# The low halves of w_in formed on TensorE instead of VectorE, in a re-planned order (mLSTM, gated MLP and routed attention on one core)

## The chip, the cores and the metric

The kernel runs on 1 core of one Trainium2 chip. The metric is the time of one execution in microseconds of device time; of the kernel before there are three timed runs. On the core, TensorE multiplies matrices into PSUM, VectorE (DVE), ScalarE (ACT) and GpSimd (POOL) work on tiles, and SyncE (SP) and ScalarE issue the loads. Each engine runs its own instructions strictly in order and waits on semaphores for the others.

## The reference, cut to what matters

Three layers in a row, on 4 batches of 768 positions.

```
# 1 mLSTM, 8 heads of 40: per step t
m_new = maximum(f + m, i)                   # gates in log space
C = exp(f + m - m_new) * C + exp(i - m_new) * outer(v, k);  n likewise with k
y = sigmoid(o_gate) * (C @ q) / maximum(|n . q|, 1)
# 2 gated MLP over x = y (320 wide), w_in 320 x 1024, w_out 512 x 320
u, v = split(relu(x @ w_in))                # 512 each
v_n = (v - mean) / sqrt(var + 1e-6)
gated = u * (w_spatial @ v_n + b_spatial);  x2 = gated @ w_out
# 3 four attention experts of 64, two chosen per position, causal softmax
out = sum over the chosen of w_e * (softmax(q k^T / 8) @ v) @ wo[e]
```

All arrays are float32. The change concerns `w_in` alone.

## The kernel before, in words

The sequence is cut into 24 tiles of 128 positions (4 batches of 6). For each there is an mLSTM chunk (`mlstm`, with `m_decay`, `m_value`, `m_state`), a normalization (`norm`, which multiplies by the v half of w_in) and an attention tile (`attend`). The gated MLP (`gmlp`) and the projections (`qkv`) work on units of one to three tiles.

Products that need more than float16 precision are made of two float16 halves: an array `t` is kept as `hi = float16(scale * t)` and `lo = float16(scale * t - hi)`, and three products stand for one. The weights get their halves in the kernel. `w_in` and `w_out` come as 8-byte words and are made into float32 by three bit instructions of VectorE (`load_f64`, tile `u`); then `split_w` makes the halves: a cast on an engine chosen by a letter (`sw`), then one subtraction on VectorE (`less`), which writes the low half.

```
    def split_w(k, t, hi, lo, scale, tag="vn"):
        yield on("sw", k)
        on("sw", k).cast(hi, t, scale)
        yield dve
        x = P - lo.shape[0]
        less(lo, t[x:], hi[x:], scale)
        flow.done(tag)
```

The ten pieces of w_in have the numbers k = 0 to 9. Pieces 0 to 7 go straight into the tile `wi` (256 columns each). Pieces 8 and 9 hold the last 64 rows of w_in packed on 128 partitions; their halves go to the tile `ee`, and four loads each by SP carry them from there into `wi`.

The order of the work is written out by hand: every coroutine (a thread such as PM3 for `mlstm(3)` or PI4 for a piece of w_in) yields the engine of its next step, and the table ORDER says which thread goes on next. The instructions of each engine come out in that order. The table CFG has one letter per step for steps that more than one engine can do: v for VectorE, a for ScalarE, p for GpSimd. All instructions are recorded in one helper, so they carry line 154 in the profile, and are told apart by their tiles. `g` is a PSUM bank (four, and two lent ones), `qs` and `qkT` are the stacked queries and keys and their transpose, `dd` the decay matrix, `cf` and `cs` the mLSTM state and its halves, `wx` and `vx` the values, `wsT` the halves of w_spatial, `qkst` early on the halves of the other weights, `vn` loads and normalized values, `u` the assembled float32 pieces and later the first half of the MLP. The first product of VectorE with the gate (`u<-pst,u`) needs the normalized tiles of the whole first batch.

Of the kernel before, what the change touches and what calls it, by code (L numbers as in the profile page):

```python
# [20 lines left out]
P = 128  # L21
# [172 lines left out]
class Flow:  # L194
# [106 lines left out]
    def run(self):  # L301
# [20 lines left out]
    qt="vaaaaaaavaaa",  # L322
    fe="p",
    ic="a",
    cc="aaaa",
    nc="aava",
    gk="vaaa",
    gt="av",
    rz="p",
    bh="pa",  # L330
    sw="avaaapapaaapvvapapaaavvappapvaapapa",
    qkh="ppavaaaaaapvvaaaaaaaaaaaavppppaaaaapavaaaaaaaaaa",
    wf="vvvvp-vvvvv-ppvvp-vvvvv",
    wh="pvaaa-avaaa-aaapa-avvap",
    wl="pvvvp-vvpvv-vpvpv-ppvpp",
    ch="aaaaa-vaava-papaa-vaaaa",
    cl="vvvpp-vvvvv-vvppv-pvvvp",
    cm="-vpvv--pppv--pvvv--vvpp",
    y="vvpvvvvvvvvvpvvppvpvvpvv",
    x1h="apvaaavavavvppavpaaaavvv",  # L340
    x1l="vvvvvpvvvppvppvvpvpvvvvv",
    w2="avavaaaa",
    vnh="aaaaavvpapvaaaaaaaaavaaa",
    ru="vvaavavvavaaaavavaaaavvvaaavavvvvaav",
    vh="------avvavaaaapaaavavva",
    Wh="------------aaaaaaaapaapaaaaaaavaaaaaaaaaaaaaaaa",
    gh="aapaapppvaaaaaaaavvvavppvvvvpapvvppa",
    qh="vavaaaaaaavvaaavvvaavvvaaaaavaaaaaaa",
    vvh="avvavvvavavaavvvvaaaaavv",
    rt="pppvvvpvp",  # L350
    ah="aaaaaapaappvavaaaaapaaapapvvaaavvapapvvpaapvaaaavvpvavavaaaavppppavvpaaapaapvaapavpvvaappavpvpav",
    osh="aavvaaapaaaapapvvaappppv",
    res="aaaavvaavvavavavvvvvavaa",
# [6 lines left out]
    al="ppppvvppvvvpppvvvvvppvvvvvvvpppvpvvvvvvpvvvvpvpvvppppppvvvvvvppvvvpppvppvppppvpppvpvvppvppvppvpv",  # L360
    co="ppppvvpvvvpppvpppvpvppvp",
    dn="ppvvpvvvppvpppppppvppvpv",
    gl="vvppvvpvvpvppvvvvpvpvvpvvvpvpppvvvpp",
    osl="ppvvvvvvvppppvppppppvvvv",
    pc="vpvvaa",
    pl="pp-vv",
    r3="vpvvppppp",
    r4="ppvppvppp",
    se="vpppvppvpvppvppvppvppppv",
    vnl="pppvvpvvpvpvvpppvvpvpppv",  # L370
# [15 lines left out]
FW6 PK1 FH7 PL4 FM2 PS1 PS0 FW7 PN1 PS0 FW7 PS3 PM3 FM2 PN1 FM3 PI1 PS2 PK1 PM5 PS2 FS11 PM3 PN0 PK2 FS11 PL4 PM5
PK0 PM3 FS10 PM2 PN0 PM3 PV4 PV5 PT4 FM3 FX11 PM3 FS10 PM3 PK1 FX11 FX10 PR0 PD4 FH8 PI0 FX10 FH9 PM3 PK3 PM3 PD4
PI0 FH9 PM5 PK4 PL6 FM5 PM3 FH8 PK0 FH9 PM3 PM3 PK3 FH8 PK2 PV4 PM3 FW8 PK4 FW9 PV4 PN2 FW8 PL5 PR0 FM3 FW9 PM3 PN1
FM3 PK2 PS0 FM4 PS5 PK3 PM6 PM4 PG1 FS13 PI0 FM4 PN2 FS12 FS13 PN2 FS12 PM4 PI0 PL5 PN0 FM4 PN3 PU0 PM6 PM4 PU0 PK4
PN1 PM4 FG0 PG1 PM4 PN3 PM4 PD5 PM4 PM4 FH10 FH11 PS3 PL7 PG1 FH10 PM4 PD5 FH11 PS0 FG1 PM4 PM4 FH10 FG0 FM4 FH11  # L390
PG1 PN3 FW10 PM4 FW11 FG2 PT5 PN2 FW10 PL6 PR0 FW11 PM4 FM4 PN2 PM5 PS1 PN2 PM7 PG1 PN3 FG1 FS14 FG2 PG1 PS5 PM5
FS15 FG0 FS14 PM5 PN2 FG3 PV6 PT6 PL6 PM5 PN3 PG1 PM5 PS2 FS15 PU0 PG1 PM5 PR0 PM7 FP6 PM5 PS2 FG3 PD6 PM5 FH12 FH13
FP6 FT1 FH12 PD6 PM5 FG1 FH13 FT1 FH12 PM5 PN3 FH13 PM5 FW12 PL8 PV6 FW13 PM5 FW12 PN4 PV6 FW13 FW12 PL7 PV6 FW13
FW12 PM5 FG0 PR0 FW13 FG1 PN4 PG1 FR6 PN3 PM6 PN4 PG1 FM6 PM6 PN4 FG3 PM6 FG0 PM6 PM6 PM8 FG2 PN4 PM6 PV7 PN5 PL7
PM6 FS17 FP7 FU3 PM6 PM6 FS16 PM6 PN4 FS16 FG1 PL8 PG1 PU1 FP7 FG3 FM6 PM6 PS3 PN5 FG2 PD7 PN4 FH14 FH15 PG1 FG1
FH14 PV7 PD7 FG2 FU4 FH15 FM6 FH14 FG3 PN5 FS17 FW14 PG1 FH15 FG2 FW14 PN5 FW15 FG0 PL8 FW14 FW15 PN6 PM8 FW14 FW15
FM6 PN5 PG1 FG3 PT7 PV7 FW15 PN6 PD8 FH16 PN5 FR7 FH16 PM7 PV7 PL9 PN5 FH17 FU5 PM7 FH17 PD8 FG3 FH16 PM7 PN6 FM7
FH17 PM7 PG1 FG3 PV8 FP8 PM7 FW16 PM7 PG1 FP8 FG1 FW16 FM7 FG2 PM7 PV8 FW17 FG3 PM7 FG2 PV8 FG4 FW16 PM7 FM7 PV8 PM7
# [103 lines left out]
def mlstm_gmlp_moe(ctx: ExitStack, tc, qkvo, i_gate, f_gate, w_in, w_in3, w_sp, b_sp, w_out, w_out3, wqkv, wo, out):  # L502
# [33 lines left out]
    def on(what, x):  # L536
        return flow.pick(what, x)
# [124 lines left out]
    def first(it):  # L662
# [883 lines left out]
    for j in range(2):  # L1546
        flow.add(gates(j), "PG", j)
# [81 lines left out]
```

## Time and profile before

| what | value |
|---|---|
| median of 3 timed runs | 522.73 us (520.88 to 523.87) |
| the profiled execution | 520.49 us, span 518.8 us |
| mean granted clock of TensorE | 0.974 of 2.4 GHz |
| TensorE, VectorE, ScalarE, GpSimd busy | 91%, 87%, 63%, 54% of the span |
| mean DMA rate | 145 GB/s |

The span is the time from the first to the last instruction of the profiled execution. An engine is busy where one of its instructions runs; TensorE's records are pipelined, so that a product's own duration is longer than the time by which it moves TensorE on. In rows with `out<-in` the tile that is written stands first.

### The profile page before, as it was taken

The page shows a single profiled execution, that of the slowest core. Times are in us where ns is not written, and L with a number is a line of the kernel's source. Part 1 is how long each engine was busy: PE and PEld are TensorE (multiplying, and loading weights), DVE is VectorE, ACT ScalarE, POOL GpSimd, SP SyncE. Part 2 cuts the span into 40 slices and gives each one's busy share as a digit, 9 for nine tenths or more (in the row PEclk, how much of TensorE's full clock was granted, in tenths as well). Part 3 has the DMA queues.
Part 4 walks back from the last instruction along what each step waited for, and adds up shares of the span by engine and source line. Part 5 has one row for each costly group of instructions (what it writes and reads, how often), then busy time and mean ns, then how long its engine had stood idle before and what let it go on. Part 6 is the DMA issues. An engine that isn't in the chain of part 4 may idle for free.

```text
span 518.8 us, 14355 instructions
## 1 busy us (share of the span) xinstructions
PE 473.5 (91%) x5409; PEld 345.6 (67%) x5409; DVE 450.9 (87%) x1164; ACT 324.6 (63%) x788; POOL 282.7 (54%) x446
## 2 busy tenths in 40 slices
PE   3575888899999999999999999999999999999895
PEld 2574566566666677666766676667775767788784
DVE  6999999989989899988988999999998866468994
ACT  2567576885565786776568675576647643335684
POOL 6554455554454768653746565356646634345671
PEclk9857899999999999999999999999999999999999
DMA  6666535652646999798977898897946946657821
GB/s 217 198 191 190 143 100 115 157 114 56 127 105 140 156 203 174 171 178 163 194 141 151 150 196 132 145 165 158 175 104 130 151 90 118 148 126 166 163 74 39
DMA packets 167803, 75.39 MB, mean 145 GB/s; under 512 B 147844, under 2 KB 157238, under 8 KB 167734
## 3 DMA queue, kind: packets, MB, share of 16 engines
q1 hardware_dynamic: 162382, 66.47, 64.3%
q10 hardware_dynamic: 5352, 8.01, 5.0%
q8 instruction: 42, 0.69, 0.5%
q14 instruction: 27, 0.22, 0.2%
HBM read 24.45 MB, written 4.52 MB: 56 GB/s over the span
## 4 chain that ended last, share of the span: by engine, by line
PE 60%; DVE 28%; issue 4%; ACT 3%; DMA 2%; POOL 1%; ACTq 0%; SPq 0%; DVEq 0%; POOLq 0%
PE g L154 57%; DVE u L154 3%; PE pst L154 3%; DVE qs L154 2%; DVE dd L154 2%; DVE ahl L154 2%; DVE vo L154 2%; DVE num L154 1%; DVE aT L154 1%; DVE g L154 1%; ACT vn L154 1%; DVE pst L154 1%; DVE Wl L154 1%; DVE vv L154 1%; DVE wsT L154 1%
## 5 line engine op out<-in xcount | busy, mean ns | idle before, releaser
L154 PE MATMUL g<-wsT,vn 128*128 128x384 f16 (+2 forms) x612 | 94.6, 307 | 0.1
L154 PEld LDWEIGHTS <-vn 128*128 128x128 f16 x648 | 59.0, 98 | 30.7 <-issue 0.2
L154 POOL TENSOR_SCALAR_AFFINE_SELECT dd<-dd 128x512 f32<-128x512 f32 x48 | 40.8, 858 | 49.2 <-ACT dd L154 48.1
L154 POOL TENSOR_TENSOR ahl<-ee,ahl 128x256 f16<-128x256 f32 (+5 forms) x46 | 49.0, 1069 | 17.8 <-DVE ahl L154 7.6
L154 ACT ACTIVATE ee<-g,sm 128x128 f32<-128x128 f32 (+3 forms) x64 | 33.4, 523 | 27.0 <-DVE sm L154 12.6
L154 PE MATMUL g<-x1T,wi 128*128 128x384 f16 (+2 forms) x288 | 46.6, 308 | 3.0 <-DVE num L154 2.8
L154 PE MATMUL g<-wi,x1T 128*128 128x512 f16 x192 | 46.8, 387 | 2.4 <-DVE num L154 1.0
L154 PE MATMUL g<-gT,w_h 128*128 128x384 f16 (+2 forms) x288 | 47.6, 308 | 0.0
L154 ACT ACTIVATE ee<-pst,sm 128x640 f32<-128x640 f32 (+1 forms) x32 | 27.0, 845 | 32.1 <-DVE sm L154 24.1
L154 PEld LDWEIGHTS <-qkst 128*128 128x128 f16 x424 | 34.6, 97 | 17.0 <-issue 1.8
L154 ACT ACTIVATE vn<-vn,nt 128x512 bf16<-128x512 f32 (+1 forms) x48 | 36.5, 762 | 6.0 <-POOL nt L154 5.4
L154 PEld LDWEIGHTS <-qs 128*128 128x128 f16 (+1 forms) x576 | 24.9, 115 | 19.8 <-issue 6.6
L154 DVE SCALAR_TENSOR_TENSOR dd<-g,dd 128x512 f32<-128x512 f32 x48 | 32.2, 681 | 6.4 <-PE g L154 5.7
L154 PEld LDWEIGHTS <-wi 128*128 128x128 f16 x288 | 26.0, 98 | 17.4 <-DVE num L154 3.6
L154 DVE CUSTOM_DVE_ANT_0 pst<-pst,mask 128x640 f32<-128x640 f32 (+1 forms) x32 | 28.6, 895 | 10.2 <-PE pst L154 10.1
L154 DVE TENSOR_TENSOR ahl<-ee,ahl 128x384 f16<-128x384 f32 (+5 forms) x50 | 35.0, 705 | 1.8 <-ACT ahl L154 1.5
L154 PEld LDWEIGHTS <-w_h 128*128 128x128 f16 x288 | 26.4, 98 | 13.3 <-issue 0.2
L154 PE MATMUL g<-qkst 128*128 128x384 f16 (+4 forms) x224 | 34.8, 288 | 0.3 <-DVE num L154 0.2
L154 DVE CUSTOM_DVE_ANT_0 g<-g,mask 128x256 f32<-128x256 f32 (+3 forms) x64 | 31.1, 492 | 3.7 <-PE g L154 3.6
L154 PE MATMUL g<-vv,aT 128*128 128x64 f16 x1008 | 33.8, 193 | 0.0
L154 PEld LDWEIGHTS <-aT 128*128 128x128 f16 x1008 | 32.6, 98 | 1.1 <-issue 0.2
L154 PEld LDWEIGHTS <-x1T 128*128 128x128 f16 x192 | 18.2, 99 | 21.9 <-issue 3.4
(228 smaller groups left out, 1293.7 us busy)
## 6 DMA issues: line engine op xcount, KB each, us to landing
vo<-in_qkvo_dram SPq DMA_DIRECT2D x24, 324.0 KB, 3.1
qkf<-in_qkvo_dram SPq DMA_DIRECT2D x24, 320.0 KB, 3.7
qkst<-qkh SPq DMA_DIRECT2D x14, 288.0 KB, 3.4
out_dram<-res SPq DMA_DIRECT2D x24, 160.0 KB, 3.9
qkst<-qkh SPq DMA_DIRECT2D x16, 192.0 KB, 2.8
vn<-in_w_in_dram ACTq DMA_DIRECT2D x10, 256.0 KB
vn<-in_w_sp_dram ACTq DMA_DIRECT2D x12, 192.0 KB, 2.3
qkst<-qkh SPq DMA_DIRECT2D x16, 96.0 KB, 3.7
```

Of the source, the lines that this page charges most:

```text
L154: r = f(*args, **kw)
```

## The change: what it does

For the pieces k = 0 to 9 the subtraction is taken off VectorE. TensorE multiplies the float32 piece by the float32 identity into a PSUM bank, and adds the product of the float16 high half with a new constant, `nident`, the identity times -1/256 (the scale of w_in is 256). The bank then holds the part of the piece that the high half lacks, and a cast with the scale 256, on an engine chosen by the new letters `lw`, writes the low half. Eight of these letters are a, two are v. `nident` is made once by ScalarE, in a new thread PX4. The other weights are split as before.

All letters of CFG and the table ORDER are new. The constants of TIM are unchanged but for the new LW.

```diff
 CFG = dict(
+    lw="aavvaaaaaa",
-    qt="vaaaaaaavaaa",
+    qt="vaaaaaavvaaa",
...
-TIM = dict(NQ=6, NE=3, NF=6, NP=2, NX=21, last=(0, 1, 2, 3, 4, 5), units=((3, 3), (3, 3), (3, 3), (3, 2, 1)))
+TIM = dict(LW=(0, 1, 2, 3, 4, 5, 6, 7, 8, 9), NQ=6, NE=3, NF=6, NP=2, NX=21, last=(0, 1, 2, 3, 4, 5), units=((3, 3), (3, 3), (3, 3), (3, 2, 1)))
...
+    nident = cp.tile([P, P], F16, name="nident")
...
+    def negative():
+        yield act
+        act.activation(nident, ident_h, AF.Copy, scale=-2.0 ** -8)
+        flow.signal("ni", 0)
...
     def split_w(k, t, hi, lo, scale, tag="vn"):
         yield on("sw", k)
         on("sw", k).cast(hi, t, scale)
+        if k in TIM["LW"]:
+            yield pe, "g", ("ni", 0)
+            pl = bank(t.shape[-1])
+            pe.matmul(pl, ident, t, start=True, stop=False)
+            pe.matmul(pl, nident, hi, start=False, stop=True)
+            flow.done(tag)
+            yield on("lw", k)
+            on("lw", k).cast(lo, pl, scale)
+            flow.done("g")
+            return
         yield dve
         x = P - lo.shape[0]
         less(lo, t[x:], hi[x:], scale)
         flow.done(tag)
...
+    flow.add(negative(), "PX", 4)
```

Three places of the new order. The first is VectorE while it assembles w_in, before the first products of the second chunk. Before:

```order
L154 SCALAR_TENSOR_TENSOR wi<-u,wi 128x256
L154 TENSOR_SCALAR u<-vn 128x256
L154 SCALAR_TENSOR_TENSOR u<-vn,u 128x256 x3
L154 SCALAR_TENSOR_TENSOR dd<-g,dd 128x512
L154 TENSOR_SCALAR u<-vn 128x256
L154 SCALAR_TENSOR_TENSOR dd<-g,dd 128x512
L154 SCALAR_TENSOR_TENSOR qkst<-vn,qkst 128x512
L154 TENSOR_TENSOR vx<-vo,w_c 128x328
L154 SCALAR_TENSOR_TENSOR wi<-u,wi 128x256
L154 SCALAR_TENSOR_TENSOR u<-vn,u 128x256
L154 SCALAR_TENSOR_TENSOR ee<-u,ee 128x256
```

VectorE at the same place now:

```order
L154 SCALAR_TENSOR_TENSOR u<-vn,u 128x256
L154 SCALAR_TENSOR_TENSOR qs<-qkf,qs 128x8x40 x2
L154 TENSOR_SCALAR u<-vn 128x256
L154 SCALAR_TENSOR_TENSOR u<-vn,u 128x256
L154 SCALAR_TENSOR_TENSOR dd<-g,dd 128x512
L154 TENSOR_SCALAR wsT<-vn 128x384
L154 SCALAR_TENSOR_TENSOR u<-vn,u 128x256
L154 TENSOR_SCALAR u<-vn 128x256
L154 SCALAR_TENSOR_TENSOR wsT<-vn,wsT 128x384
L154 SCALAR_TENSOR_TENSOR u<-vn,u 128x256
L154 SCALAR_TENSOR_TENSOR dd<-g,dd 128x512
```

The subtractions into `wi` and `ee` are gone; the assembly of `u`, the halves of `wsT` and the decay products `dd` stand closer together.

The second is TensorE around the small product of a gate row with ones (`aT,ones`), in the first chunk. Before:

```order
L154 MATMUL g<-qkT 128x128
L154 LDWEIGHTS qkT
L154 MATMUL g<-qkT 128x128
L154 MATMUL g<-aT,ones_83 128x96
L154 LDWEIGHTS qs
L154 MATMUL g<-wx,qs 128x41
```

TensorE at the same place now:

```order
L154 MATMUL g<-wx,qs 128x41
L154 MATMUL g<-vo,dd 128x41 x8
L154 MATMUL g<-u,ident 128x256
L154 LDWEIGHTS nident
L154 MATMUL g<-wi,nident 128x256
L154 MATMUL g<-aT,ones_84 128x96
L154 LDWEIGHTS qkT
L154 MATMUL g<-qkT 128x128
```

The second of the ten new pairs stands ahead of the gate product and of a group of key products (`qkT`).

The third is ScalarE at the first high half of w_in. Before:

```order
L154 ACTIVATE wi<-u 128x256
L154 ACTIVATE qkT<-g 120x1024
L154 ACTIVATE vo<-vo 128x320
L154 DMA vn<-in_w_in_dram 128x512
L154 ACTIVATE qkT<-g 120x1024
L154 DMA vn<-in_w_out_dram 128x512
L154 ACTIVATE qkst<-vn 128x512
L154 ACTIVATE wi<-u 128x256
```

ScalarE at the same place now:

```order
L154 ACTIVATE wi<-u 128x256
L154 DMA vn<-in_w_out_dram 128x512
L154 DMA vn<-in_w_sp_dram 128x384
L154 ACTIVATE qkT<-g 120x1024 x2
L154 ACTIVATE wi<-g 128x256
L154 ACTIVATE dd<-g,i_c 128x128 x4
L154 ACTIVATE ee<-u 128x256
```

The cast of the high half (`wi<-u`) and that of the low half out of PSUM (`wi<-g`) stand on either side of two copies of 1024 columns.

## Rows read from the trace of the kernel before

**Rows 1.** The page's busy time, share of the span and instructions of each engine.

```profile
PE 473.5 (91%) x5409; PEld 345.6 (67%) x5409; DVE 450.9 (87%) x1164; ACT 324.6 (63%) x788; POOL 282.7 (54%) x446
```

**Rows 2.** Windows: stretch, length, then busy time (instructions) of each engine, clock, DMA share.

```profile
6.00:20.00 14.00, 8.07 (x57) 7.29 (x57) 11.28 (x27) 5.36 (x16) 9.18 (x14) 1.00 0.80 239
20.00:45.00 25.00, 16.17 (x162) 15.25 (x163) 24.90 (x66) 14.99 (x40) 11.69 (x13) 0.65 0.61 177
45.00:60.00 15.00, 10.72 (x96) 7.52 (x96) 14.52 (x37) 9.21 (x20) 6.68 (x11) 0.73 0.62 161
60.00:104.00 44.00, 38.72 (x415) 27.45 (x414) 42.98 (x101) 32.48 (x74) 23.14 (x36) 0.98 0.54 126
104.00:124.00 20.00, 19.19 (x187) 12.30 (x186) 16.88 (x42) 14.81 (x33) 10.68 (x17) 1.00 0.41 93
124.00:480.00 356.00, 350.32 (x3983) 250.10 (x3982) 308.30 (x811) 220.91 (x553) 196.63 (x311) 1.00 0.78 149
480.00:518.80 38.80, 30.29 (x519) 25.64 (x516) 29.26 (x84) 25.31 (x53) 19.67 (x29) 1.00 0.41 93
```

**Rows 3.** The page's chain by engine; then its pieces: start, length, what.

```profile
PE 60%; DVE 28%; issue 4%; ACT 3%; DMA 2%; POOL 1%; ACTq 0%; SPq 0%; DVEq 0%; POOLq 0%
...
98.90 0.61 DVE dd L154
...
114.81 2.98 PE g L154 x56
...
123.03 1.19 DVE u L154 x3
```

**Rows 4.** VectorE's groups by form: names, shapes, count; busy us, mean ns; idle before.

```profile
L154 DVE TENSOR_TENSOR cs<-cf,cs 80x328 f16<-80x328 f32 x14 | 7.4, 531 | 0.6 <-ACT cs L154 0.6
...
L154 DVE TENSOR_SCALAR vv<-g 128x256 f16<-128x256 f32 x13 | 5.3, 411 | 0.2 <-PE g L154 0.2
...
L154 DVE SCALAR_TENSOR_TENSOR wi<-u,wi 128x256 f16<-128x256 f32 x8 | 3.3, 417 | 0.0
...
L154 DVE TENSOR_TENSOR sm<-cw,sm 128x4 f32<-128x4 f32 x9 | 2.4, 270 | 0.0
...
L154 DVE SCALAR_TENSOR_TENSOR ee<-u,ee 128x256 f16<-128x256 f32 x3 | 1.8, 604 | 0.0
```

**Rows 5.** Timeline of VectorE at 28 us: start, length, instruction.

```profile
27.99 0.42 DVE L154 SCALAR_TENSOR_TENSOR wi<-u,wi 128x256 f16<-128x256 f32 x1
28.32 0.42 DVE L154 SCALAR_TENSOR_TENSOR u<-vn,u 128x256 uint32<-128x256 uint32 x1
```

**Rows 6.** TensorE: two stretches of the timeline, then a group by form.

```profile
14.27 2.87 PE L154 MATMUL g<-f_e,ident 96*128 96x128 f32 x24
...
36.32 2.77 PE L154 MATMUL g<-f_e,ident 96*128 96x128 f32 x16
...
L154 PE MATMUL g<-wsT,vn 128*128 128x256 f16 x72 | 8.5, 273 | 0.0
```

**Rows 7.** Waits of VectorE before 115 us: for whom, us, times, longest.

```profile
DVE qkT L154 <- PE g L154: 1.2, 1, 1.2
...
DVE dd L154 <- PE g L154: 0.6, 2, 0.4
```

**Rows 8.** ScalarE's group by form: the cast of 256 columns out of PSUM.

```profile
L154 ACT ACTIVATE vv<-g 128x256 f16<-128x256 f32 x11 | 4.2, 379 | 7.4 <-PE g L154 7.2
```

**Rows 9.** Timeline of TensorE from 46 us; idle time before a row in brackets.

```profile
46.97 1.00 PE L154 MATMUL g<-wx,qs 128*128 128x41 f16 x24 [5.26 <-DVE wx L154]
...
52.20 1.47 PE L154 MATMUL g<-wi,x1T 128*128 128x512 f16 x6 [0.31 <-DMA wi<-ee]
```

**Rows 10.** Timeline of ScalarE: a copy of 1024 columns out of PSUM.

```profile
23.82 1.02 ACT L154 ACTIVATE qkT<-g 120x1024 f16<-120x1024 f16 x1
```

**Rows 11.** Timeline at 79 us: VectorE's cast, and GpSimd beside it.

```profile
79.15 1.82 DVE L154 TENSOR_SCALAR wi<-u 128x256 f16<-128x256 f32 x1
...
78.55 2.27 POOL L154 TENSOR_TENSOR vn<-vn 128x512 f16<-128x512 f32 x2
```

More of the change, by code (lines that the diff above doesn't have):

```diff
@@ L321 @@
 CFG = dict(
-    qt="vaaaaaaavaaa",
-    fe="p",
+    lw="aavvaaaaaa",
+    qt="vaaaaaavvaaa",
+    fe="a",
     ic="a",
-    cc="aaaa",
-    nc="aava",
-    gk="vaaa",
+    cc="aaav",
+    nc="aaav",
+    gk="aaaa",
     gt="av",
     rz="p",
[L330 to L353, printed above, removed]
+    bh="aa",
+    sw="aaavpaaaaaaaaapaaapaaaavpaavavaaapa",
+    qkh="vpvaaavaaaaavapaaaaaaaavaapaaaaaaaaaaavaaavaaaaa",
+    wf="pvvvp-vvvvp-pvvvv-vpvvv",
+    wh="avvav-aaaap-paavp-aaaaa",
+    wl="pvvvp-vvppp-pvvpv-vpvpv",
+    ch="avvpa-vavaa-aaaaa-avaaa",
+    cl="ppvvp-vppvp-vvvpv-ppppp",
@@ new lines @@
+    cm="-vvvp--pvvp--pvvp--vppv",
+    y="vpppvvvvvvpvvpvvvvvpvvvv",
+    x1h="aaaaaavaaavaaaaapavaavap",
+    x1l="vpvvvpvvppvvppvvvvvvvvvv",
+    w2="vavaavav",
+    vnh="paavaavaaapaaavaaaaaaaaa",
+    ru="avvaaaaaavaaaaaaaaaaaaavavavaavaavvv",
+    vh="------paaaavvapvvavaapaa",
+    Wh="------------aaaaaaaaaaavvavaaapaaaaaaapappaaavpa",
+    gh="aaaaaavaaaaavaaaaaappavpavavvapaaavp",
+    qh="aaaaaaaaaaavvavaaavaaaaaavvaaaaaavav",
+    vvh="vvaaaaaaavaaaavvvavaaaaa",
+    rt="vpvvvvppv",
+    ah="pvpavvpaavpvaappvaaaaapaaavpavppvaaaapaaaaavvaavppvvaapvpaapvavppaavvpaapvpapaavvvaaaaavapapvaav",
@@ L360 @@
[L360 to L370, printed above, removed]
+    to="----------------------va",
+    Wl="------------vvvvvvvvpvpvpvvvvvpvpvvvvppvvvvvvvvv",
@@ L371 @@
+    al="vvvvvvpvvvpvpvpvpvvvvpvvpvvvvvpvpvvpvppvvpvvvppvpppvpvpvppvpvvpppppvppvvpvvppvppvppvvppvvppppppv",
+    co="vvppvvvvpppvvvvvvvvvvvpv",
+    dn="vpvvvvvvppvppppvvvvpvvvv",
+    gl="pvvpppvvvppppvvvvvpvvppvpppvvvvvpvvv",
+    osl="pvpvppvvppvpppvvpvppvvvv",
+    pc="vvvaaa",
+    pl="vv-vv",
+    r3="vvvvvpvvp",
+    r4="pvppvpppp",
+    se="pppppvvppvvvpvvvpvvpvppv",
+    vnl="ppvvvpvppvpvvvpppvvvpvpp",
 )
-TIM = dict(NQ=6, NE=3, NF=6, NP=2, NX=21, last=(0, 1, 2, 3, 4, 5), units=((3, 3), (3, 3), (3, 3), (3, 2, 1)))
+TIM = dict(LW=(0, 1, 2, 3, 4, 5, 6, 7, 8, 9), NQ=6, NE=3, NF=6, NP=2, NX=21, last=(0, 1, 2, 3, 4, 5), units=((3, 3), (3, 3), (3, 3), (3, 2, 1)))
@@ L394 @@
[L394 to L398, printed above, removed]
@@ new lines @@
+PN4 PM6 PG1 FS16 PD7 PN5 FH14 FH15 PN4 FG0 FH14 PD7 FU4 FG2 FM6 FH15 FH14 FG3 PN5 FH15 FW14 PG1 PN5 FW14 FW15 FG1
+FW15 FW14 PN6 PL8 PV7 FW15 PM8 FW14 PV7 FW15 PN5 FG3 FM6 PN6 FR7 PM7 PV7 PN5 PG1 PD8 FH16 PR0 PM7 FH16 FG1 PN5 PL9
+PM7 FH17 PM7 FM7 FH17 PD8 FH16 FG1 PM7 PG1 PV8 FP8 PM7 FH17 FG2 PM7 PN6 FP8 FW16 FG3 FM7 PR0 FW16 FG3 PV8 FW17 FW16
+FG4 PM7 PV8 PM7 FG3 PV8 FG0 PM7 PM7 FM7 FG2 FG3 PM9 PM7 FS19 FG1 FG0 FW16 PL9 FS18 FG3 FW17 FG0 PM7 FG2 PG1 FG1 FW17
+PN6 FG5 FG0 FG1 FG2 FG0 FW17 FG4 PU0 FM8 FM7 FG1 FR8 PG1 PM8 PT8 FS18 PN6 FS19 FG6 FM7 PT9 PV9 PL9 FG2 FM8 PM9 PM8
@@ new lines @@
+FH33 FQ11 FH32 PT16 FQ11 FH33 FQ9 PM15 PN14 FM15 PA3 PQ2 PQ2 FP16 FM15 PA4 PN14 FW32 PA5 FP16 FW33 FM15 PM15 PV16
+FV6 PM17 FW33 PV16 PV16 FV7 PA4 PA3 FV6 FS35 PM15 PN14 FW33 PM15 FM16 PA4 FW32 PM15 FV8 PM15 FM16 FW32 PM15 FE23
+PM15 FG15 FW33 FV8 PN13 PM15 FW32 FV8 PM15 PM15 PU3 PN13 PM15 FG15 FR16 FV7 PA4 FM16 FM15 PA6 PA7 PA8 FS34 PL17 FV7
+FE24 PM15 PM16 FV6 PA4 FM16 FE25 FE26 FO2 FE27 FO2 PU4 PM16 FE24 PA4 FE26 FE24 FE25 PM16 FE24 FE28 FM16 FE25 PA5
+PM16 FE24 FE28 PM16 FE26 FS35 FE25 FS34 PV17 PL17 FO2 PM16 FE25 PN15 PM17 PN13 FE28 FE27 FG13 FE26 PA5 FE26 FO2 PA5
```

237 lines of the change are left out of this document (116 added, 121 removed).

## The prediction, made before the changed kernel ran

> **What bounds the kernel now.** I read the busy totals first. TensorE works 473.5 us of a span of 518.8, VectorE 450.9, ScalarE 324.6, GpSimd 282.7 [rows 1]. A sum of that kind hides stages, so I cut the span in windows [rows 2]. The reader is to see three stages there. From 20 to 104 us VectorE is full (24.90 of 25, 14.52 of 15 and 42.98 of 44 us) while TensorE has gaps: 8.8, 4.3 and 5.3 us, 18.4 us in all. From 104 to 480 us TensorE is full (19.19 of 20 and 350.32 of 356). In the last 38.8 us neither is, TensorE is idle for 8.5. So the kernel begins as a VectorE kernel and goes on as a TensorE kernel. The chain of waits agrees: by engine it is 60% TensorE and 28% VectorE, and the place of the change-over can be read in it. Up to 98.90 us its pieces are VectorE's; then ScalarE and GpSimd finish the normalization of the first batch's last tiles, and from 114.81 us TensorE carries the chain [rows 3]. What makes VectorE full in the first stage is the preparation of weights, which lies beside the first mLSTM chunks: the bit assembly of w_in and w_out (three instructions a piece) and the low halves (one a piece).
>
> After the change-over TensorE has the same products to do before and after. So a microsecond taken from VectorE's stage before the first gate product shortens the whole run, as long as TensorE, ScalarE and the loads keep pace; one taken from VectorE behind it is mostly hidden under TensorE.
>
> **Term 1, low halves that leave VectorE.** Eight subtractions into wi and two of the three into ee go (pieces 0 to 9 of the splits; the third ee is w_out's and stays). Their rows say 417 and 604 ns a piece [rows 4]. But a duration includes an overlap with the next instruction: one started at 27.99 us and the next at 28.32 [rows 5]. VectorE moves on by 0.33 us each. Ten times 0.34 is 3.4 us; by durations it would be 4.5, the far end.
>
> **Term 2, what comes back.** Two of the ten casts go to VectorE (the two v of the new letters). The nearest row is the cast of 256 columns out of PSUM into float16, 411 ns [rows 4], at the same overlap 0.34 us: 0.7 us. Terms 1 and 2: -2.7 us.
>
> **Term 3, other letters before the first gate product.** Counted in the order, VectorE has 270 instructions before its first product with the gate (now at 123.03 us [rows 3]) and will have 259. Eight fewer are terms 1 and 2; three more leave in a mixed exchange (casts of 0.28 to 0.38 us and two output products leave, a 1024 column copy out of PSUM and two gate subtractions come). I put that at -0.2 us, between -1 and +0.5.
>
> **Term 4, TensorE.** Ten pairs are added: a float32 product of 256 columns by the identity, a float16 product by the negative identity. No such pair is in the trace. The nearest float32 rows are the decay products of 128 columns: the code issues 24, the trace has 48 records of them, so two a product. 24 records take 2.87 us at a granted clock of 1.00 (2.4 GHz) and 16 take 2.77 us in the stretch with a mean of 0.65, between that level and 1.2 GHz [rows 2, 6]: 0.24 and 0.35 us a product of 128 columns, 0.48 and 0.69 for 256. The float16 half: 72 products of 256 columns took 8.5 us, 0.12 us each at the upper clock [rows 6], at most double at the lower. A pair is 0.60 to 0.93 us, ten are 6 to 9 us. They lie in the first stage, where TensorE has 18.4 us of gaps [rows 2], and are hidden there in sum. They aren't hidden where VectorE waits for a product: it did so for 1.8 us before 115 us [rows 7], against 73.7 us of TensorE work up to 104 us [rows 2]. Another 8 us at the same share cost 0.2 us. If the cover were gone they would cost all of 6 to 9.
>
> The Trainium skill has a rule that speaks against the change. The page "FP8 and Floating Point Precision", section TensorE Precision Notes, says that a true FP32 product takes four passes through the array. The decay products agree (0.24 us for 128 columns, where four passes at 2.4 GHz are an estimate of 0.21). By the rule a float32 product here would be 0.43 us, or 0.85 at 1.2 GHz, the ten 4 to 9 us, and the sum would stay as it is, since the gaps hold that too.
>
> **Term 5, ScalarE and waits.** ScalarE takes six casts into wi, two into ee, one for the negative identity, and other letters: in all 685 instructions become 723, GpSimd goes from 451 to 411, VectorE from 1166 to 1169. A cast of 256 columns out of PSUM is 379 ns there [rows 8]; eight are 3.0 us. ScalarE works 32.48 of 44 us from 60 to 104 [rows 2], so there is room, and I cost it at nothing in the sum. The waits that are added: a pair on TensorE stands behind the high half's cast on ScalarE, and its result waits on ScalarE's queue. Behind the second pair stand a gate product and the four-head key products, for which VectorE's decay multiplication waits. Of the pieces that go through ee, a later low half also moves the four loads of wi that SP issues from it; the first products of x1 and wi waited 0.31 us for such a load [rows 9]. The chain gets longer by a pair and a cast, less one subtraction, about 0.9 us, once for each of two pieces. TensorE waited 5.26 us for VectorE just before, at 46.97 us [rows 9], so there is slack and I take 0, at worst 1.
>
> **Term 6, behind the change-over.** VectorE has 14 instructions more there, but smaller ones: for example six low halves of the state leave it (531 ns) and nine products of 4 columns come (270 ns) [rows 4]. Taking the forms whose counts change at their means, I estimate 3 us less work. TensorE has 5.7 us of idle time from 124 to 480 us [rows 2], which is all that could be had. At the chain's 28% for VectorE it is -0.8; ScalarE's extra work there takes half of that: -0.4, between -3 and +2, since every row of the order moves a little.
>
> **Sum.** -3.4 + 0.7 - 0.2 + 0.2 + 0 - 0.4 = -3.1 us. The profiled execution took 520.5 us (span 518.8 and 1.7 around it); it would become 517.4. It lies 2.2 us under the median of the timed runs, 522.73, which spread from 520.88 to 523.87. I forecast against the median: 519.6 us. What a measurement can tell from no change is about 0.5%, 2.6 us: faster means under 520.1, slower over 525.3.
>
> **Rivals.** *Nothing arrives (522.5).* ScalarE and TensorE are the next to be late: the end of the stage, 98.90 to 114.81 us, is already a chain of ScalarE and GpSimd [rows 3], and ScalarE has some 5 us more to do before it, the changed forms at their means. For it: the saving is small beside that chain. Against it: that chain starts from VectorE's last multiplication at 98.90, and moves with it.
>
> *Slower (526).* The ten pairs stall TensorE in its own order. Each needs a high half that ScalarE casts between other work. A copy of 1024 columns there holds the queue for 1.02 us [rows 10], and in the new order the first pair's high half and its low half stand on either side of two of these. If each pair waits 0.65 us on average, ten wait 6.5; the key products and the state products behind them are late by as much, and with them the decay multiplications and the whole first stage. Less the 3.1 that is 3.4 us above the median. It decides against the change from 0.31 us a pair. Against it: TensorE was waiting for VectorE in this stage anyway, up to 5.26 us at one place [rows 9], and a stall inside such a wait costs nothing.
>
> *More than forecast (516.8).* Some VectorE instructions take much longer when GpSimd works: a cast of 256 columns into wi took 1.82 us beside two GpSimd subtractions of 2.27 us [rows 11], where its like takes about 0.4. GpSimd loses 40 instructions, and the ten subtractions that read two SBUF tiles are replaced by reads of PSUM. If two such collisions go, 2 times 1.4 us come on top: 516.8. The Trainium skill's page "SBUF — State Buffer", section SBUF: two separate sides, has it as a rule: VectorE and GpSimd share a port pair, held for a whole instruction by VectorE operations with two SBUF inputs among others, and the loser blocks. The trace agrees, with the 1.82 us. Against it: the order is new everywhere, and new collisions come as easily as old ones go.
>
> **How the numbers follow.** Forecast 0.45, nothing arrives 0.23, slower 0.17, more 0.15. The forecast's own range is 517.5 to 522 (terms 1 to 3 by their ends, and the spread of the medians). The range of 515 to 525 takes in the larger gain and most of the no-gain case and leaves out half of the slower one. Faster by over 0.5%: 0.65 of the forecast, nearly all of the larger gain, a little of the second: 0.47. Slower: most of the third and a little of the second: 0.17. Between them 0.36.
>
> **What would show it.** In the profile after, VectorE's share from 20 to 104 us stays near full, its instructions for wi fall from 9 to 3, and VectorE's first product with the gate comes some 3 us before its 123.03 us of now [rows 3]; TensorE's busy time in the first 104 us grows by 6 to 9 us and its waits for VectorE shrink. Wrong would be: pairs that wait for ScalarE by over 0.3 us each, a first stage of the same length with VectorE idle in it, or a change that lies behind 124 us.

## The result, and the profile after

The changed kernel takes 525.51 us, the kernel before in the same comparison 522.14 (medians of 18 runs each): a ratio of 1.0061, 95% interval 1.0037 to 1.0084. By the ratio that is 3.2 us slower, on the opposite side of the forecast of 519.6 and just outside its range of 515 to 525. (The ratios leave out runs that count as disturbed, among them one of these 18 and two of E1's nine, so they are not exactly the quotients of the medians.)

The totals moved much as worked out. This is the page's line of busy time after the change:

```profile
PE 482.2 (92%) x5439; PEld 349.7 (67%) x5439; DVE 443.8 (85%) x1167; ACT 337.8 (65%) x826; POOL 270.5 (52%) x406
```

Against [rows 1] TensorE has 8.7 us more, VectorE 7.1 less. By stages (stretch, length, busy us of PE, PEld, DVE, ACT, POOL, then granted clock, DMA share, GB/s):

```profile
6.00:20.00 14.00, 10.80 (x61) 10.02 (x61) 10.95 (x29) 5.46 (x18) 6.09 (x5) 1.00 0.76 207
20.00:45.00 25.00, 17.81 (x180) 14.69 (x179) 22.21 (x61) 18.19 (x48) 9.74 (x12) 0.83 0.71 206
45.00:60.00 15.00, 10.59 (x99) 7.11 (x99) 12.92 (x35) 9.85 (x26) 8.07 (x10) 0.84 0.58 144
60.00:104.00 44.00, 40.08 (x368) 28.26 (x367) 37.22 (x84) 28.71 (x65) 22.29 (x35) 0.92 0.47 103
104.00:124.00 20.00, 18.10 (x218) 11.84 (x217) 16.62 (x40) 16.31 (x39) 8.04 (x14) 1.00 0.54 125
124.00:480.00 356.00, 351.16 (x3965) 249.60 (x3963) 308.98 (x818) 231.78 (x577) 192.61 (x288) 1.00 0.74 148
```

Compare with [rows 2]: VectorE is no longer full in the first stage (37.22 of 44 us where it was 42.98), and TensorE's clock from 60 to 104 us is 0.92 where it was 0.98, with 47 fewer products done. What VectorE saved is idle time, and the stage is longer. Up to 104 us TensorE has 5.6 us more than before (79.3 in the first four rows, 73.7 in [rows 2]); 6 to 9 were forecast. VectorE's first product with the gate comes at 126.82 us, 3.8 after its 123.03 before, where the prediction had it 3 earlier. Behind it nothing has changed: the rest takes 395.4 us, before 395.8.

The chain of waits, by engine and then its pieces (start, length, what), shows the place:

```profile
PE 63%; DVE 17%; DMA 6%; ACT 5%; issue 4%; POOL 4%; SPq 1%; ACTq 0%; DVEq 0%; POOLq 0%
...
76.36 3.35 DVE xs L154
79.71 0.61 DVE dd L154
...
80.45 11.55 PE g L154 x91
```

VectorE's share fell from 28% [rows 3] to 17%, but one subtraction holds the chain for 3.35 us. The timeline there (start, length, instruction; in brackets the idle time before it and what ended it), sorted by engine:

```profile
75.18 4.53 DVE L154 TENSOR_TENSOR xs<-vo,xs 128x64 f16<-128x64 f32 x2
79.63 1.27 DVE L154 SCALAR_TENSOR_TENSOR dd<-g,dd 128x512 f32<-128x512 f32 x2
92.35 1.06 DVE L154 TENSOR_TENSOR xs<-vo,xs 128x64 f16<-128x64 f32 x2 [1.57 <-ACT xs L154]
...
126.82 1.01 DVE L154 TENSOR_TENSOR u<-pst,u 128x384 f32<-128x384 f32 x2
...
75.55 0.81 POOL L154 TENSOR_TENSOR wx<-vx,wx 128x328 f16<-128x328 f32 x1
76.46 0.74 POOL L154 TENSOR_TENSOR cf<-cf,f_b 80x328 f32<-80x328 f32 x1
77.16 2.26 POOL L154 TENSOR_TENSOR vn<-vn 128x512 f16<-128x512 f32 x2
...
43.52 1.19 PE L154 MATMUL g<-u,ident 128*128 128x256 f32 x2 [1.71 <-DVE u L154]
80.45 0.77 PE L154 MATMUL g<-wx,qs 128*128 128x41 f16 x24 [3.29 <-DVE dd L154]
81.06 3.61 PE L154 MATMUL g<-vo,dd 128*128 128x41 f32 x16
84.47 1.20 PE L154 MATMUL g<-u,ident 128*128 128x256 f32 x2
85.46 0.42 PE L154 MATMUL g<-wi,nident 128*128 128x256 f16 x1
...
85.92 0.38 ACT L154 ACTIVATE wi<-g 128x256 f16<-128x256 f32 x1 [6.04 <-PE g L154]
```

Two subtractions `xs`, which take 1.06 us at 92.35, take 4.53 us at 75.18: beside them GpSimd runs four instructions with two SBUF inputs almost back to back, to 79.42 us. Behind `xs` on VectorE stands the decay multiplication `dd`, which frees the PSUM banks, and TensorE waits 3.29 us for it. Then TensorE comes back at a lower clock: the windows after the change say 0.61 and 0.71,

```profile
75.00:80.00 5.00, 2.16 (x16) 0.96 (x13) 5.00 (x4) 4.51 (x12) 4.46 (x8) 1.00 0.19 51
80.00:85.00 5.00, 4.55 (x41) 4.53 (x42) 4.04 (x11) 0.00 (x0) 0.99 (x3) 0.61 0.46 104
85.00:90.00 5.00, 5.00 (x35) 2.61 (x34) 3.38 (x10) 2.06 (x6) 0.00 (x0) 0.71 0.51 96
```

and those of the kernel before, in the same stretch, 1.00:

```profile
80.00:85.00 5.00, 3.29 (x35) 2.03 (x35) 5.00 (x11) 1.14 (x6) 0.81 (x1) 1.00 0.29 58
85.00:90.00 5.00, 4.96 (x43) 3.34 (x42) 4.90 (x13) 4.04 (x12) 2.78 (x6) 1.00 0.56 126
```

So the 16 decay products take 3.61 us, the pair behind them 1.4 (84.47 to 85.88), and ScalarE, whose queue holds the pair's cast, stands idle for 6.04 us.

A measure of the place is the time between the starts of the outputs `vo<-vo,den` of the fourth and the sixth tile, read from VectorE's timeline of each profiled execution (us; E1 to E12 are the experiments in their order below):

| kernel | ratio to before (95%) | tile 1 | tile 4 | tile 6 | 4 to 6 | span |
|---|---|---|---|---|---|---|
| before | 1 | 37.31 | 74.13 | 96.32 | 22.19 | 518.8 |
| after | 1.0061 (1.0037-1.0084) | 35.04 | 72.22 | 100.99 | 28.77 | 522.2 |
| E1 | 0.9922 (0.9893-0.9951) | 34.52 | 72.93 | 96.69 | 23.76 | 517.9 |
| E2 | 0.9956 (0.9930-0.9982) | 34.46 | 71.25 | 95.59 | 24.34 | 517.6 |
| E3 | 1.0000 (0.9979-1.0021) | 35.02 | 71.41 | 99.49 | 28.08 | 519.2 |
| E4 | 1.0112 (1.0074-1.0151) | 40.47 | 79.54 | 102.25 | 22.71 | 526.2 |
| E5 | 0.9953 (0.9934-0.9972) | 36.02 | 72.63 | 96.46 | 23.83 | 517.8 |
| E6 | 1.0050 (1.0023-1.0076) | 33.08 | 69.37 | 100.01 | 30.64 | 520.8 |
| E7 | 0.9952 (0.9922-0.9981) | 38.18 | 75.23 | 98.29 | 23.06 | 520.4 |
| E8 | 1.0069 (1.0045-1.0093) | 37.70 | 76.72 | 99.41 | 22.69 | 522.8 |
| E9 | 0.9955 (0.9929-0.9981) | 35.32 | 71.88 | 95.63 | 23.75 | 515.8 |
| E10 | 0.9956 (0.9928-0.9984) | 34.91 | 73.72 | 99.13 | 25.41 | 519.8 |
| E11 | 1.0036 (1.0010-1.0062) | 37.56 | 76.59 | 98.46 | 21.87 | 521.0 |
| E12 | 1.0004 (0.9974-1.0034) | 35.60 | 71.92 | 96.02 | 24.10 | 517.6 |

The kernel after is 1.9 us ahead at the fourth tile and 4.7 us behind at the sixth. The times of the tiles are those of one execution of each kernel.

### The profile page after: what moved, and what is told of

Same layout as the page of the kernel before. It is cut to its first block, busy times and chain, and to the rows that moved or that the text cites. A ratio compares the mean times of both kernels' runs of the same rounds, so it can differ in the third digit from the quotient of the medians.

```text
span 522.2 us, 14430 instructions
## 1 busy us (share of the span) xinstructions
PE 482.2 (92%) x5439; PEld 349.7 (67%) x5439; DVE 443.8 (85%) x1167; ACT 337.8 (65%) x826; POOL 270.5 (52%) x406
## 4 chain that ended last, share of the span: by engine, by line
PE 63%; DVE 17%; DMA 6%; ACT 5%; issue 4%; POOL 4%; SPq 1%; ACTq 0%; DVEq 0%; POOLq 0%
PE g L154 60%; PE pst L154 2%; DVE u L154 2%; DVE dd L154 2%; DMA oT<-os 2%; DVE ahl L154 1%; POOL nt L154 1%; DVE aT L154 1%; DMA aT<-ahl 1%; DVE qs L154 1%; DMA x1T<-xs 1%; DVE xs L154 1%; DMA rows<-r_dram 1%; DVE pst L154 1%; DMA aT<-in_i_gate_dram 1%
## 5 line engine op out<-in xcount | busy, mean ns | idle before, releaser
L154 POOL TENSOR_TENSOR ahl<-ee,ahl 128x384 f16<-128x384 f32 (+5 forms) x45 | 51.1, 1138 | 27.8 <-ACT ahl L154 20.7
L154 POOL TENSOR_SCALAR_AFFINE_SELECT dd<-dd 128x512 f32<-128x512 f32 x48 | 34.9, 739 | 48.7 <-ACT dd L154 48.4
L154 DVE CUSTOM_DVE_ANT_0 g<-g,mask 128x128 f32<-128x128 f32 (+3 forms) x64 | 30.8, 495 | 5.5 <-PE g L154 5.2
L154 DVE TENSOR_TENSOR ahl<-ee,ahl 128x128 f16<-128x128 f32 (+5 forms) x51 | 33.7, 661 | 0.4 <-ACT ahl L154 0.4
L154 PEld LDWEIGHTS <-x1T 128*128 128x128 f16 x192 | 18.4, 100 | 22.0 <-issue 2.9
L154 POOL TENSOR_SCALAR nt<-nt 128x1 f32<-128x1 f32 x48 | 18.6, 388 | 26.0 <-ACT vn L154 22.5
```

Of the source, the lines that this page charges most:

```text
L154: r = f(*args, **kw)
```

## Experiments

**E1, the GpSimd half of the collision.** The changed kernel, two letters:

```diff
-    vnl="ppvvvpvppvpvvvpppvvvpvpp",
+    vnl="vvvvvpvppvpvvvpppvvvpvpp",
```

> The changed kernel with one edit: two letters of vnl (0 and 1) go from p to v, so that the two 128x512 subtractions vn<-vn that GpSimd runs at 77.16 us (2.26 us for both) are VectorE's, behind the gate selections. Theory (the loss is one collision of VectorE and GpSimd at 75 to 80 us): VectorE's two xs subtractions of line 154, which took 4.53 us there, end by about 77 us, TensorE's gate product g<-wx,qs comes some 2 us earlier and its granted clock stays at or near 1.00 from 80 to 90 us; two subtractions of about 0.6 us come on VectorE. The fifth tile's output (vo<-vo,den, 89.43 us in the changed kernel) starts 3 to 5 us earlier and the time is 520 to 522 us. Rival (the ten identity pairs and their waits cost the time): the tile starts at 89 us or later, and the time stays at 525 to 527.

Measured: 0.9922, faster than both kernels. VectorE's timeline:

```profile
75.89 1.59 DVE L154 TENSOR_TENSOR xs<-vo,xs 128x64 f16<-128x64 f32 x2
77.40 1.28 DVE L154 SCALAR_TENSOR_TENSOR dd<-g,dd 128x512 f32<-128x512 f32 x2
```

`xs` takes 1.59 us, the clock from 80 to 90 us is 1.00, the sixth tile comes 4.3 us earlier. As the theory said, and more.

**E2, the VectorE half.** The changed kernel, one letter:

```diff
-    x1l="vpvvvpvvppvvppvvvvvvvvvv",
+    x1l="vpvpvpvvppvvppvvvvvvvvvv",
```

> The changed kernel with one edit: letter 3 of x1l goes from v to p, so that the two xs subtractions that were blocked for 4.53 us on VectorE run on GpSimd, behind what GpSimd has there. VectorE goes straight on to the gate selections dd. Theory (VectorE blocked at this place is what costs): dd starts about 3 us earlier, TensorE's gate product follows at about 77.5 us, the clock stays up, the fifth tile's output comes 3 to 4 us earlier and the time is 521 to 523 us; GpSimd ends its part of the stage 1 to 2 us later, which can take some of it back. Rival (pairs): no change of the fifth tile's start beyond 1 us and a time of 525 to 527.

Measured: 0.9956, a median of 519.39 us, better than the 521 to 523 expected. The collision is still there, with another victim:

```profile
74.35 1.29 DVE L154 SCALAR_TENSOR_TENSOR dd<-g,dd 128x512 f32<-128x512 f32 x2
76.09 3.62 DVE L154 TENSOR_TENSOR cs<-cf,cs 80x328 f16<-80x328 f32 x1
...
77.08 2.27 POOL L154 TENSOR_TENSOR vn<-vn 128x512 f16<-128x512 f32 x2
...
76.33 0.76 PE L154 MATMUL g<-wx,qs 128*128 128x41 f16 x24
```

`cs` (531 ns on average, [rows 4]) is blocked for 3.62 us, almost as long as `xs` was. But `dd` has gone before it, TensorE has its bank and over 3 us of work, and the time is 5.5 us less than after the change. What a collision costs is set by what stands behind the blocked instruction.

**E3, the new order without pairs.** The changed kernel; the step of the pair and that of the cast become one subtraction and an empty step:

```diff
         if k in TIM["LW"]:
-            yield pe, "g", ("ni", 0)
-            pl = bank(t.shape[-1])
-            pe.matmul(pl, ident, t, start=True, stop=False)
-            pe.matmul(pl, nident, hi, start=False, stop=True)
+            yield dve
+            less(lo, t, hi, scale)
             flow.done(tag)
-            yield on("lw", k)
-            on("lw", k).cast(lo, pl, scale)
-            flow.done("g")
+            yield dve
             return
```

> The changed kernel with the ten low halves back on VectorE as subtractions of float32 piece and float16 half, no identity products and no casts of them; the new order and letters are kept. Theory (the pairs gain, the new order loses): VectorE gets 2.7 us of work back before its first gate product, so the tiles up to 72 us start about 2 us later than in the changed kernel, the loss at 75 to 90 us may shift since everything before it shifts, and the time is 525 to 529 us. Rival (the pairs cost the time, the order is as good as the old): TensorE loses 6 to 9 us of work and ScalarE the casts, and the time falls to 519 to 522 us.

Measured: 1.0000, the rival's number. The collision is in this kernel as well, so the block belongs to the order and not to the pairs (VectorE's timeline, then two windows):

```profile
74.37 4.52 DVE L154 TENSOR_TENSOR xs<-vo,xs 128x64 f16<-128x64 f32 x2
...
75.00:80.00 5.00, 1.72 (x22) 0.79 (x20) 5.00 (x4) 3.70 (x10) 4.36 (x7) 1.00 0.18 51
80.00:85.00 5.00, 5.00 (x52) 4.12 (x49) 4.78 (x14) 0.88 (x2) 0.27 (x1) 0.60 0.45 103
```

VectorE finishes four instructions in 5 us, and the clock falls to 0.60. But this kernel has no loss against the kernel before: the loss takes the collision and the pairs together, since E1 and E2 defuse the one, E3 takes out the other, and the loss is gone each time. My expectation that the pairs gain in every order was wrong; whether they gain without the collision is asked in E5.

**E4, the pairs in the old order.** The kernel before with the pair and its cast where the subtraction stood:

```diff
...
+    nc.vector.tensor_scalar(nident, ident, -2.0 ** -8, None, op0=ALU.mult)
...
+        if k < 10:
+            yield pe, "g"
+            pl = bank(t.shape[-1])
+            pe.matmul(pl, ident, t, start=True, stop=False)
+            pe.matmul(pl, nident, hi, start=False, stop=True)
+            on("lw", k).cast(lo, pl, scale)
+            flow.done(tag, "g")
+            return
         yield dve
```

> The kernel before, in its own order and letters, with the ten low halves formed by the identity pairs and cast with the new letters lw (eight on ScalarE, two on VectorE); a pair and its cast stand where the subtraction stood in the row of the order. Theory (the pairs gain by themselves): the tiles up to 72 us start 1 to 2.5 us earlier than in the kernel before, no new collision at 75 to 80 us, and the time is 519 to 521.5 us. Rival (the pairs cost): the first tiles start later, TensorE shows waits for ScalarE of 0.3 us or more a pair and the time is 523.5 to 527.

Measured: 1.0112; the theory fails here. The first tile is 3.2 us late, and the timeline says why:

```profile
33.02 0.29 DVE L154 TENSOR_SCALAR u<-vn 128x256 uint32<-128x256 uint32 x1 [3.51 <-issue]
...
28.31 3.62 PE L154 MATMUL g<-vo,dd 128*128 128x41 f32 x16
31.72 1.20 PE L154 MATMUL g<-u,ident 128*128 128x256 f32 x2
```

The second pair stands behind 16 decay products at half clock. It reads a buffer `u`, and VectorE's bit assembly, which needs that buffer, starts as the pair's float32 product ends (32.92 us): VectorE, the engine that was to be relieved, waits 3.51 us for TensorE.

**E5, neither collision nor pairs.** E1 with the edit of E3.

> The first experiment's kernel (vn<-vn on VectorE, so no collision at 75 to 80 us) with the ten low halves back on VectorE as subtractions and no identity pairs. It prices the pairs where the collision does not decide. The theory as changed by the first four runs (the pairs gain where the order gives them room on TensorE, and lose where TensorE's queue is in the way; the collision hides that): 2.7 us more on VectorE before its first gate product, so 1.5 to 3 us slower than the first experiment's 517.2 (0.9922 of the kernel before), a ratio of 0.995 to 0.998. Rival (the pairs lose everywhere, as 1.0061 against 1.0000 with and without them in the new order says at face value): 2 to 3 us faster than with pairs, a ratio of 0.986 to 0.989.

Measured: 0.9953, as expected. Against E1's 0.9922 the pairs gain 0.3%, 1.6 us, but that is not clear of zero: the two intervals overlap from 0.9934 to 0.9951, and the quotients of the medians are 0.9955 for E1 and 0.9956 here. The new order without collision does gain 2.5 us on the old one without any pair. The pairs change TensorE's clock too; these are E5 and then E1:

```profile
20.00:45.00 25.00, 18.92 (x158) 18.02 (x158) 22.77 (x62) 17.03 (x44) 8.52 (x9) 0.52 0.62 188
...
20.00:45.00 25.00, 18.59 (x178) 15.88 (x179) 22.86 (x63) 17.49 (x46) 9.51 (x12) 0.80 0.68 194
```

**E6, the clock apart from the wait.** The changed kernel; nothing reads the added products:

```diff
...
+        if n == 4:
+            for _ in range(56):
+                pe.matmul(lent["fill"][:, 384:512], ident_h, ident_h, start=True, stop=True)
         qs, wh, wl = m["qs"], m["wh"], m["wl"]
```

> The changed kernel with 56 extra float16 products of the identity by itself (128 columns, into unused columns of a PSUM bank) in TensorE's queue right ahead of the fifth tile's gate product g<-wx,qs: they fill the wait of 77.2 to 80.4 us, and nothing reads them. The collision stays. Theory (half of the loss is the granted clock that falls to 0.61 and 0.71 after TensorE's wait): the wait for dd is as long, but the clock stays at 1.00 from 80 to 90 us, the decay products take 2.0 instead of 3.61 us, the fifth tile's output starts 2.5 to 3.5 us earlier than 89.43 us and the time falls by 2 to 3.5 us to 521 to 523. Rival (the clock costs nothing, all of the loss is the delay of the selections): the output starts at 89 us or later and the time is 524.5 to 527.

Measured: 1.0050, not told apart from the changed kernel's 1.0061; the time is nearer the rival's. TensorE's timeline shows both halves of the answer:

```profile
74.15 3.29 PE L154 MATMUL g<-ident_h 128*128 128x128 f16 x56
...
78.21 1.96 PE L154 MATMUL g<-vo,dd 128*128 128x41 f32 x16
...
83.71 3.60 PE L154 MATMUL g<-wi,x1T 128*128 128x512 f16 x8 [2.53 <-DMA x1T<-xs]
```

The decay products take 1.96 us instead of 3.61, and from the fourth tile to the fifth 2.4 us are won. Then TensorE waits 2.53 us for the transposing load `x1T<-xs`, which starts from the same late `xs`, and the clock falls there instead (3.60 us for eight products that took 1.89 at 72 us). The late `xs` has two followers; in the changed kernel the slow clock hid the second.

**E7, both letters.** E1 and E2 together.

> The changed kernel with both letter edits of the first two experiments: the two vn<-vn subtractions on VectorE, the two xs subtractions on GpSimd. With either alone the ratio was 0.9922 and 0.9956. If the collision's delay of the gate selections is all that either removes, the second adds only its 0.5 us of VectorE time: 0.990 to 0.994, 516 to 518 us. Rival (each removes something of its own, the wait behind the collision and the collision itself): 0.986 to 0.990.

Measured: 0.9952, above both expectations. From the fourth to the sixth tile this kernel takes 23.06 us, the shortest of the new order, but its first tile came at 38.18 us, with the very program that had it at 33.08 to 35.04 in the kernels after, E1, E2 and E6. TensorE at that place:

```profile
26.64 3.62 PE L154 MATMUL g<-vo,dd 128*128 128x41 f32 x16
30.05 1.20 PE L154 MATMUL g<-u,ident 128*128 128x256 f32 x2
```

In this execution the clock was still down (in E1 the same products took 1.96 and 0.68 us), so the second pair began 2.6 us later than in E1 (27.47), and VectorE waited 3.2 us for products at `dd`.

**E8, eight pairs in the old order.** E4 with the second and third piece left to VectorE:

```diff
-        if k < 10:
+        if k < 10 and k not in (6, 9):
```

> The kernel before with pairs in its own order as in the fourth experiment (1.0112), but the second and third piece there keep their subtraction on VectorE: their pairs stood behind 16 decay products at half clock (31.72 and 32.93 us), and VectorE's bit assembly waited 3.51 us at 33.02 us for the buffer u that the second pair reads. Theory (what costs in the old order is that wait, the other eight pairs gain or are neutral): the first tile's output starts at 37 us as in the kernel before, not at 40.47, and the ratio falls to 1.000 to 1.005. Rival (every pair costs its share, 0.6 us each): eight of ten pairs cost 4.7 us, a ratio of 1.008 to 1.010.

Measured: 1.0069, between the two. The first tile is back at 37.70, so those two pairs cost the 3 us; the other eight still lose 2.2 us up to the third tile (63.65 against 61.07). From 37 to 64 us VectorE waits there 1.6 us for ScalarE, whose casts of low halves wait 4.0 us for TensorE, and 1.2 us for something that the trace doesn't name; in the kernel before its waits in this stretch are 0.4 us.

**E9, seven pairs in the new order.** E1 with `LW=(0, 1, 2, 3, 5, 7, 8)`; the other three are subtractions.

> The first experiment's kernel (0.9922) with the first three pairs in TensorE's order left out: these three low halves (two for wi, one for ee) are VectorE subtractions again, seven pairs stay. In one of the executions seen (the kernel with both letters) TensorE ran at half clock from 24 to 35 us, these three pairs took 1.6 us each instead of 0.9 and the first tile's output came at 38.18 us; in others the clock was up again by 26 us and it came at 33.1 to 35.0. Theory (the early pairs stretch what VectorE waits for when the clock is late): the runs lie closer together than the first experiment's 515.6 to 519.7 and the late first tile does not occur; 1 us more work on VectorE; the ratio stays within 0.990 to 0.995. Rival (the early pairs pay like the others): 0.995 to 0.997.

Measured: 0.9955 (516.55 to 522.98 us): no narrower, and an interval that covers both theories. It decides nothing.

**E10, the early clock held up.** E1 with idle products that nothing reads, in `mlstm`:

```diff
...
+                if (n, x) == (1, 1):
+                    for _ in range(40):
+                        pe.matmul(full[:, :P], ident_h, ident_h, start=True, stop=True)
```

> The first experiment's kernel with 40 float16 products of the identity by itself (128 columns, nothing reads them) in TensorE's queue ahead of the second tile's query and key transposes, where it waited 2.7 us for VectorE's qs at 19 to 22 us after which its granted clock fell to about 0.64. Theory (the early pairs and decay products cost more in executions where the clock is down there): the clock stays at 1.00 from 20 to 30 us, the decay products at 26 us take 1.96 us in every execution, the first tile's output starts at 33 to 34.5 us and the ratio is 0.986 to 0.991. Rival (the early clock is off the path, VectorE sets the end there): first tile at 34.5 or later, 0.991 to 0.995.

Measured: 0.9956; the first tile at 34.91. The clock is 1.00 from 20 to 30 us as wanted, and nothing is gained over E1: the rival's first tile, and a ratio just above the rival's.

**E11, the same in the old order.** E4 with 72 such products.

> The kernel before in its own order with all ten pairs (1.0112), and 72 such extra products ahead of the second tile's transposes, where TensorE waited 5.0 us up to 22.48 us. Theory (in the old order the pairs cost because they stand behind 16 decay products at half clock, 3.62 us, and VectorE's bit assembly waits for the buffer u that the second pair reads): with the clock up the decay products take about 2 us, the second pair ends 2.5 us earlier, VectorE's wait of 3.51 us falls to 1 us or less, the first tile starts at 37.5 to 38.5 instead of 40.47 us and the ratio falls to 1.004 to 1.008. Rival (the clock does not decide it, the place in the queue does): wait and ratio stay, 1.009 to 1.013.

Measured: 1.0036, a little better than expected. The timelines of TensorE and VectorE:

```profile
26.93 2.09 PE L154 MATMUL g<-vo,dd 128*128 128x41 f32 x16
...
30.12 0.48 DVE L154 TENSOR_SCALAR u<-vn 128x256 uint32<-128x256 uint32 x1 [1.69 <-ACT dd L154]
```

The products take 2.09 us instead of 3.62, VectorE's wait falls from 3.51 to 1.69, the first tile comes at 37.56. About two thirds of what E4 loses is gone (0.8 of 1.1%, +/- 0.5). That this part was the clock in front of the pairs fits, but isn't shown: the old order with the added products and without pairs was not run.

**E12, E10 without pairs.** E5 with the 40 products.

> The kernel without pairs and without the collision (0.9953) with the same 40 extra products ahead of the second tile's transposes. It separates the clock from the pairs: against the kernel with pairs and the same products it prices the pairs at a clock that is held up. Theory: without pairs TensorE is seldom what VectorE waits for at 20 to 35 us, so the products change it little, 0.993 to 0.996, and the pairs are worth 2 to 4 us at a clock held up. Rival (the clock is worth the same with and without pairs): 0.990 to 0.992.

Measured: 1.0004, slower than expected. Its profile (span 517.6, where E5 has 517.8) doesn't show why, and that stays open. E10 is 0.5% faster, but that is not the price of the pairs at one clock, as was wanted, because here the products didn't hold the clock up:

```profile
25.00:30.00 5.00, 3.58 (x18) 3.50 (x18) 4.93 (x14) 2.95 (x11) 1.00 (x2) 0.68 0.37 117
30.00:35.00 5.00, 4.62 (x46) 4.10 (x45) 5.00 (x15) 3.95 (x9) 0.98 (x3) 0.50 0.69 193
```

In E10 both of these stretches have 1.00.

## Why the prediction was wrong

**The step that failed is term 3**, and with it the sum: "Counted in the order, VectorE has 270 instructions ... and will have 259", priced at -0.2 us, between -1 and +0.5. I counted which instructions leave VectorE and not beside whom the others now stand. The order itself is worth more than I gave it where nothing collides (E5: -2.5 us with term 6, forecast -0.6). But it brings one collision of VectorE and GpSimd ahead of the decay multiplication, and that costs 1.4% or 7.3 us by the ratios of the kernel after and E1 (+/- 1.9; 5.7 by the quotients of their medians, 4.3 by the spans of their profiles). With the -1.6 from E5 to E1 the three ratios add up to the measured +3.2, as they must. The sum had no term for such a collision.

The price stood in my own rows: a cast of 1.82 us beside the same two GpSimd subtractions [rows 11]. I used it only for collisions that go (the rival "more than forecast") and put the other sign in half a sentence, "new collisions come as easily as old ones go", without a place or a price. Before the change, that collision hit a cast behind the decay multiplication, which had started at 76.77 us, so that TensorE had its products. It was not free: the chain of the kernel before passes through the cast, and TensorE waits for VectorE soon after.

```profile
79.22 1.75 DVE wi L154
...
84.79 1.47 PE L154 MATMUL g<-x1T,wi 128*128 128x384 f16 x8 [1.71 <-DVE num L154]
```

In the new order this collision, 1.4 us, is gone, which may be most of the 1.9 us that E5 gains beyond the forecast; no run isolates it. The prediction's rival cited the Trainium skill, page "SBUF — State Buffer", section SBUF: two separate sides, for a lock that lasts one instruction. The direction agrees; the size doesn't. By that rule the second `xs`, which starts as the first GpSimd instruction ends (76.36 us), would have waited for one more at most, `cf` with 0.74 us; here it ended 3.35 us later, behind all four. [rows 11] showed it already: the cast ended at 80.97, behind both GpSimd subtractions, of which the first ends near 79.7.

**Terms 1, 2 and 4 (the pairs), -2.5 us together:** not shown. In the new order without the collision the ratios say -1.6 +/- 1.8 us (E5 to E1) and -2.5 +/- 2.1 (E12 to E10, at different clocks), the quotients of the medians -0.1 and -1.1; with the collision the pairs lose 3.2 +/- 1.6 (E3 to the kernel after). In all three comparisons of profiles the fourth tile comes later with the pairs, by 0.3, 1.8 and 0.8 us, though the first comes as early or up to 1.5 earlier. And in the old order the same ten pairs lose 1.1% (E4). Term 4's rule, gaps of 18.4 us hide 6 to 9 us of work "in sum", says nothing of who waits behind a pair in its gap.

**Term 5, ScalarE and waits, 0:** right that the pairs in the kernel after don't wait for ScalarE (the largest wait of one is 1.71 us, for VectorE at 43.52). So the rival "slower", with its 526, came near the time by a mechanism that isn't there. What waits is ScalarE, 6.04 us, because the pair is late behind the collision.

**Term 6, -0.4:** the 395.4 against 395.8 us behind the first gate product agree, as far as one profile of each can tell.

**"VectorE's share stays near full"** was to show the forecast right; it fell to 37.22 of 44 us with a longer stage, which I had named as a sign of being wrong.

**Open:** why the loss takes the pairs as well. With them the collision costs 7.3 us by the ratios, 5.7 by the medians and 4.3 by the spans; without them (E3 to E5) 2.5, 2.6 and 1.4, which just takes back what the order gains, while the stretch of the fourth to the sixth tile differs by 5.0 and 4.3 us. Part of the 7.3 may be the early spread seen in E7; one profile per kernel can't settle it.

E1 has the lowest ratio of the new order, 0.9922 of the kernel before, by two letters. But E2, E5, E7, E9 and E10 (0.9952 to 0.9956) are not told apart from it, and E5 gets there without a pair.

## What to carry to other kernels

When an order is planned anew, go through the instructions with two SBUF inputs on VectorE that stand beside a run of such instructions on GpSimd, and look at what is queued behind them: a block of 4.5 us cost 4 to 7 us ahead of the products' bank, and one of 3.6 us little behind it (E2). Work moved into another engine's gaps is priced by who waits behind it there, not by the sum of the gaps, and a wait of TensorE can be paid twice: the decay products took 3.61 us behind a wait of 3.29 us, and 1.96 where it was filled (E6). A kernel whose first stage depends on that clock needs many runs, and its profile is one of several that it can show.

## What the runs showed of the hardware

VectorE did not get in at the end of the GpSimd instruction that blocked it: `xs` waited 3.35 us over three further ones (0.74 and twice 1.13 us), `cs` in E2 for as long, although a memset without inputs stands in between. In E1, with the last two gone, `xs` got in behind the first (1.59 us), and `cf` was the one to take longer (0.91 us for 0.74). These are E1's chain and GpSimd's timeline:

```profile
77.06 0.41 DVE xs L154
...
77.17 0.91 POOL L154 TENSOR_TENSOR cf<-cf,f_b 80x328 f32<-80x328 f32 x1
```

In both kernels the second `xs` starts some 0.1 us before `cf` (76.36 and 76.46 after the change), so the starts alone don't decide who goes first; what does isn't shown.

TensorE's clock comes back at different moments in executions of one program: up to there E1 and E7 are the same, and 16 decay products at 26 us took 1.96 us in E1 and 3.62 in E7; the first tile's output came between 33.08 and 38.18 us. The times go with it: of the changed kernel's 18 executions the nine with a mean granted clock of 0.975 or more took 521.99 to 525.49 us, the nine with 0.973 or less 525.53 to 530.20. Products that nobody reads kept it at 1.00 for the products behind them in E6, E10 and E11, not in E12. In E6 that moved the wait to the next late transfer, in E10 it gained nothing, in E11 the first tile came 2.9 us earlier.
